# RWKV-6 attention and a maxout layer on one core: one step loop with helpers, against a tabled order of single operations

## The chip, the cores and the metric

One core of one Trainium2 chip runs the kernel. The time is that of the device in microseconds; 199.82 is the median of three runs of the kernel before. The engines are TensorE (PE; its weight loads are PEld), VectorE (DVE), ScalarE (ACT), GpSimd (POOL) and SyncE (SP), which here issues transfers. Each engine works its own queue in order.

## The reference

```python
for t in range(S):                       # attention: B=4, H=8, S=768, D=48
    cur = np.einsum('bhd,bhe->bhde', u[None] * kt, vt)
    y[:, :, t] = np.einsum('bhd,bhde->bhe', rt, state + cur)
    state = wt[:, :, :, None] * state + np.einsum('bhd,bhe->bhde', kt, vt)
...
h1 = x @ w1                              # maxout: x is [3072, 384], w1 and w2 [384, 1024]
h2 = x @ w2
g = np.maximum(h1, h2)
return (g @ w_out).astype(np.float32)
```

Here x is the attention's y with the heads of a token side by side.

## The kernel before

The sequence is cut into chunks of 256 positions. A unit n is one chunk of one batch: chunk n // 4 of batch n % 4, so there are 12 units, and unit n needs the state that unit n-4 left. Partition p of a unit's tiles holds positions 2p and 2p+1 of the chunk.

What a unit goes through, by the names in the code:
- `load` (L80): w, k, r and v, 384 KB each, on SP's queue; 4 buffers each.
- `logw`: lw = ln w (ACT), lp = sum of the two positions (POOL). `cumsum`: one matmul with a triangle (PE, PSUM `ex`), the exponential A (ACT), mz (DVE). `exps`: A and iA (ACT). `scale_rk`: rkn, r and k times the decays (DVE).
- `bonus_mul` and `bonus_sum`: vb, rku = r k u (POOL), its row sums dg (DVE), vd (POOL).
- `transp`: 8 transposes of rkn for r and 8 for k through one PSUM buffer `tr`, and the copies rT and kT (DVE). `kv`: 32 small matmuls to PSUM `y`, then S and Tf (DVE).
- `scores`, twice: 16 matmuls to one PSUM buffer `sc` and the masked copy M (DVE). `y_inter`, `y_intra`: the output in PSUM `y`, copied to x (ACT). `xt`: transposes and the copy xT (ACT).
- `gate` j = 0 to 3: 6 matmuls of xT with wd = w1 - w2 to `go` (two PSUM buffers), a Relu to gT (ACT). With max(h1, h2) = relu(h1 - h2) + h2 the second term goes through wc = w2 w_out.
- `outp` b = 0, 1: 3 matmuls with wc and 8 with w_out, the copy osb (ACT, 4 buffers) and the store of 192 KB (SP, L368), whose target is written as two interleaved sets of 64 rows.
- `decay_row`, `decay_load`: one row of mz goes to DRAM (row, L212) and comes back spread over partitions (WL, L219); `decay_exp`, `decay`: the state S_f and S_0 of the batch (ACT, POOL).

The weights: w1 on SP (L90), w2 and w_out on POOL's queue (L137), w2 turned by three DMA transposes on SP (L145, `weights_turn`), wd by three subtractions (DVE, L141), wc by 24 matmuls (L151, `weights_out`).

The schedule is manual: an engine gets its instructions in the order in which the Python code calls the helpers. `step` lays attention of unit a (first half), unit t (second half), the gates of g and the outputs of o past one another, helper by helper; the calls at the end start the first units and then run `step(n, n-1, n-2, n-2)`. A helper holds the work of several engines, so their orders are bound to one another.

Of the kernel before, what the change touches and what calls it, by code (L numbers as in the profile page):

```python
# [12 lines left out]
AX = mybir.AxisListType  # L13

# [20 lines left out]
def _body(tc, r, k, v, w, u, moe_w1, moe_w2, moe_w_out, out):  # L35
    nc = tc.nc
    B, H, S, D = r.shape
    P = 128
# [9 lines left out]
    NU = NC * B  # L48

# [3 lines left out]
    ldp = tc.alloc_tile_pool(name="ld", bufs=4)  # L53
# [18 lines left out]

    L = {}

    def load(n):
        c, b = unit(n)
        d = {}
        for name, src in (("w", w), ("k", k), ("r", r), ("v", v)):
            t = ldp.tile([P, H, 2, D], F32, tag="l" + name, name="l" + name)
            nc.sync.dma_start(  # L80
                out=t.rearrange("p h i d -> p h (i d)"),
                in_=src[b, :, c * C:(c + 1) * C, :].rearrange("h (p i) d -> p h (i d)", i=2))
            d[name] = t
        L[n] = d

    load(0)
    u_b = const.tile([P, HD], F32)
    nc.sync.dma_start(out=u_b, in_=u.rearrange("h d -> (h d)").partition_broadcast(P))
    w1f = const.tile([P, KO, d_ff], F32)
    nc.sync.dma_start(out=w1f, in_=moe_w1.rearrange("(o p) n -> p o n", p=P))  # L90


# [4 lines left out]
    triI = const.tile([P, P], F32)  # L97
    mask = const.tile([P, 2, 2, Q], F32)
    sel = const.tile([P, 2, 2, Q], BF16)

    def constants():
        make_upper_triangular(nc, triI, val=1.0, diag=True)
        nc.gpsimd.memset(sel, 0.0)
        for b in range(2):
            q = slice(b * Q, (b + 1) * Q)
            for i in range(2):
                nc.gpsimd.tensor_copy(sel[q, i, i, :], ident[q, q])
                for i2 in range(2):
                    nc.gpsimd.tensor_copy(mask[q, i, i2, :],
                                          (triI if (i, i2) == (0, 1) else triS)[q, q])  # L110

    NRK = 2
    MZ = [const.tile([P, 2, H, DP], F32, name=f"mz{i}") for i in range(2)]
    rkn_b = [const.tile([P, 2, 2, H, DP], BF16, name=f"rkn{i}") for i in range(NRK)]
# [9 lines left out]
    for b in range(B):  # L124
        nc.vector.memset(S_f[b], 0.0)
    for t in S_0 + S_1:
        nc.gpsimd.memset(t, 0.0)


    wd_sb = const.tile([P, KO, d_ff], BF16)  # L130
# [5 lines left out]
    def weights_load(src, dst):  # L136
        nc.gpsimd.dma_start(out=dst, in_=src.rearrange("(o p) n -> p o n", p=P))  # L137

    def weights_gate():
        for ko in range(KO):  # L140
            nc.vector.tensor_sub(wd_sb[:, ko, :], w1f[:, ko, :], w2_sb[:, ko, :])  # L141

    def weights_turn():
        for ko in range(KO):
            nc.sync.dma_start_transpose(out=w2T_sb[:, ko], in_=w2_sb[:, ko, :])  # L145

    def weights_out():
        for ko in range(KO):
            wc_p = pt_([P, HD], F32, "go", 2)
            for fo in range(FO):  # L150
                nc.tensor.matmul(wc_p, w2T_sb[:, ko, fo, :],  # L151
                                 wo_sb[:, fo, :], start=(fo == 0), stop=(fo == FO - 1))
            nc.vector.tensor_copy(wc_sb[:, ko, :], wc_p)


    U = {}
# [4 lines left out]
    def logw(n):  # L161
        s = U[n] = {}
        s["lw"] = lw = wt_([P, H, 2, D], F32, "lw")
        nc.scalar.activation(lw, L[n]["w"], AF.Ln)  # L164
        s["lp"] = lp = wt_([P, H, D], F32, "lp")
        nc.gpsimd.tensor_add(lp, lw[:, :, 0, :], lw[:, :, 1, :])  # L166

    def bonus_mul(n):
        s = U[n]
        s["vb"] = vb = wt_([P, H, 2, D], BF16, "vb", 3)  # L170
        nc.gpsimd.tensor_copy(vb, L[n]["v"])
        s["rku"] = rku = wt_([P, H, 2, D], F32, "rku", 1)
        nc.gpsimd.tensor_mul(rku, L[n]["r"], L[n]["k"])  # L173
        nc.gpsimd.tensor_mul(  # L174
            byi(rku), byi(rku),
            u_b.rearrange("p (h d) -> p h d", h=H).unsqueeze(1).to_broadcast([P, 2, H, D]))

    def bonus_sum(n):
        s = U[n]
        dg = wt_([P, H, 2, 1], F32, "dg")  # L180
        nc.vector.reduce_sum(dg, s["rku"], axis=AX.X)  # L181
        s["vd"] = vd = wt_([P, 2, H, D], BF16, "vd", 3)
        nc.gpsimd.tensor_mul(byi_inv(vd), L[n]["v"], dg.to_broadcast([P, H, 2, D]))  # L183

    def byi_inv(t):
        return t.rearrange("p i h d -> p h i d")

    def cumsum(n):
        s = U[n]
        lw, lp = s["lw"], s["lp"]  # L190
# [9 lines left out]
    def exps(n):  # L200
        s = U[n]
        mz = s["mz"]
        nc.scalar.activation(s["A"][:, 1], mz[:, 0, :, 0:D], AF.Exp)
        s["iA"] = iA = wt_([P, 2, H, D], F32, "iA", 1)
        nc.scalar.activation(iA, mz[:, :, :, 0:D], AF.Exp, scale=-1.0)

    def decay_row(n):
        if last(n):
            return
        s = U[n]  # L210
        s["row"] = row = drp.tile([1, H * DP], F32, tag="row", name="row")
        nc.sync.dma_start(out=row, in_=s["mz"][P - 1:P, 1].rearrange("b h d -> b (h d)"))  # L212

    def decay_load(n):
        if last(n):
            return
        s = U[n]
        s["WL"] = wl = wt_([P, NP], F32, "WL")
        nc.sync.dma_start(out=wl, in_=s["row"].rearrange("b (p x) -> x (b p)", x=P))  # L219

    def scale_rk(n):
        s = U[n]
        s["rkn"] = rkn = rkn_b[n % NRK]
        nc.vector.tensor_mul(rkn[:, 0, :, :, 0:D], byi(L[n]["r"]), s["A"])
        nc.vector.tensor_mul(rkn[:, 1, :, :, 0:D], byi(L[n]["k"]), s["iA"])  # L225
# [12 lines left out]

    def decay_exp(n):
        if last(n):  # L240
            return
        s = U[n]
        s["Wt"] = wt = wt_([P, NP, 1], F32, "Wt")
        nc.scalar.activation(wt.rearrange("p q o -> p (q o)"), s["WL"], AF.Exp)

    def kv(n):

        s = U[n]
        b = unit(n)[1]
# [12 lines left out]
        for e in range(2):
            q = slice(e * DP, (e + 1) * DP)
            nc.vector.tensor_add(S_1[n % 2][q, :, e * D:(e + 1) * D],  # L264
                                 kp[q, 0, 0:NP * D].rearrange("p (q d) -> p q d", d=D), S_f[b][q])
        if not last(n):
            nc.vector.tensor_add(T_f[b].rearrange("p q d -> p (q d)"), kp[:, 1, 0:NP * D],
                                 S_f[b].rearrange("p q d -> p (q d)"))

    def decay(n):  # L270
        if last(n):
            return
        b = unit(n)[1]
# [192 lines left out]
```

## Time and profile before

| | us |
|---|---|
| median of 3 runs (199.71 to 200.17) | 199.82 |
| the profiled execution | 199.22 |
| its span, first to last instruction | 197.5 |
| PE busy / POOL / DVE / ACT | 146.2 / 101.9 / 108.3 / 88.1 |
| transfers of 8 KB and less on SP's queue: share of the 16 DMA engines' span | 49.6% |

In the profile SP's issuing of transfers is not busy time, so SP has to be read from the timeline and its waits. A DMA share is the mean over sixteen DMA engines, so two busy ones show as about 0.13. Matmul ends are modelled: a group of matmuls shows some 0.15 us longer than the distance to the next group's start.

### The profile page before, as it was taken

Reading aid. Unit: us, or ns where it says so; the run is one execution under the profiler, and the core shown is the slowest. Engines: PE = TensorE matmul, PEld = TensorE weight load, DVE = VectorE, ACT = ScalarE, POOL = GpSimd, SP = SyncE. Lnnn points to the kernel's source line nnn. Section 1 sums busy time; section 2 is a strip of 40 time slices with the busy share of each in tenths; the row PEclk is TensorE's granted clock in tenths of the full one; section 3 lists DMA queues with packets and bytes.
Section 4 is the critical chain, followed back from the end, with each engine's and each line's share of the span. In section 5 each row is a group of like instructions: output and inputs, shape, how many; then the busy total and the mean of one; then the engine's idle time right before and its main releaser. Section 6 shows DMA issues by size and latency. Waiting matters only on the chain.

```text
span 197.5 us, 4973 instructions
## 1 busy us (share of the span) xinstructions
PE 146.2 (74%) x2080; PEld 100.3 (51%) x2080; DVE 108.3 (55%) x154; ACT 88.1 (45%) x153; POOL 101.9 (52%) x115
## 2 busy tenths in 40 slices
PE   0325543674998998989989899898998989997900
PEld 0114321443566665666757667566675666755500
DVE  3245840777827758477583774847748477540000
ACT  4300122705058364583645826558365572535400
POOL 6996002996196294782946929469295642000000
PEclk9999999999699999999999999999999999999965
DMA  6995999979414826646549366473571110101110
GB/s 172 325 297 95 140 174 325 269 199 319 124 26 125 229 75 184 185 124 168 135 130 240 79 168 179 120 208 95 162 209 53 42 53 14 46 35 36 49 42 35
DMA packets 62454, 28.07 MB, mean 142 GB/s; under 512 B 57432, under 2 KB 61656, under 8 KB 62432
## 3 DMA queue, kind: packets, MB, share of 16 engines
q1 hardware_dynamic: 60992, 26.19, 49.6%
q0 software_dynamic: 1440, 1.57, 5.1%
q8 instruction: 16, 0.26, 0.5%
q14 instruction: 6, 0.05, 0.1%
HBM read 23.81 MB, written 4.73 MB: 145 GB/s over the span
## 4 chain that ended last, share of the span: by engine, by line
PE 40%; DVE 19%; POOL 9%; ACT 9%; DMA 8%; issue 6%; SPq 3%; DVEq 0%; POOLq 0%; ACTq 0%
PE go L362 13%; DVE M L291 7%; PE go L359 6%; PE go L347 5%; DMA w_sb<-in_moe_w_dram 4%; DVE S L264 4%; SPq L145 3%; DMA lw<-in_w_dram 3%; PE ex L192 3%; ACT xT L337 3%; PE sc L288 2%; ACT osb L365 2%; PE y L323 2%; DVE rkn L225 2%; PE y L302 2%
## 5 line engine op out<-in xcount | busy, mean ns | idle before, releaser
L347 PE MATMUL go<-xT,wd_sb 128*128 128x256 bf16 x288 | 38.5, 279 | 6.8 <-ACT xT L337 6.7
L183 POOL TENSOR_TENSOR vd<-lv,dg 128x768 bf16<-128x768 f32 x12 | 17.7, 1477 | 41.7 <-DVE dg L181 41.7
L347 PEld LDWEIGHTS <-wd_sb 128*128 128x128 bf16 x288 | 27.9, 100 | 16.7 <-issue 10.2
L362 PE MATMUL go<-wo_sb,gT 128*128 128x384 bf16 x192 | 35.4, 328 | 0.0
L351 ACT ACTIVATE gT<-go 128x512 bf16<-128x512 f32 x48 | 27.4, 591 | 14.4 <-PE go L347 14.2
L291 DVE TENSOR_TENSOR M<-sc,mask 128x1024 bf16<-128x1024 f32 x24 | 29.3, 1222 | 6.8 <-PE sc L288 6.7
L365 ACT COPY osb<-go 128x384 f32<-128x384 f32 x24 | 11.5, 479 | 44.7 <-PE go L362 44.7
L362 PEld LDWEIGHTS <-gT 128*128 128x128 bf16 x192 | 18.9, 99 | 12.8 <-issue 0.5
L174 POOL TENSOR_TENSOR rku<-rku,u_b 128x768 f32<-128x768 f32 x12 | 22.4, 1870 | 0.9
L166 POOL TENSOR_TENSOR lp<-lw 128x384 f32<-128x384 f32 x12 | 12.7, 1056 | 19.6 <-ACT lw L164 19.6
L173 POOL TENSOR_TENSOR rku<-lr,lk 128x768 f32<-128x768 f32 x12 | 22.4, 1866 | 0.0
L232 PE MATMUL tr<-ident,rkn 128*128 128x128 bf16 x192 | 15.5, 226 | 9.1 <-DVE rT L237 6.4
L192 PE MATMUL ex<-lp,triS 128*128 128x384 f32 x24 | 11.9, 583 | 10.7 <-POOL lp L166 10.7
L237 DVE COPY rT<-tr 128x1024 bf16<-128x1024 bf16 x12 | 8.3, 690 | 20.9 <-PE tr L232 20.9
L288 PE MATMUL sc<-rT,kT 48*64 48x128 bf16 x384 | 10.9, 231 | 11.6 <-DVE M L291 11.6
L232 PEld LDWEIGHTS <-rkn 128*128 128x128 bf16 x192 | 12.8, 101 | 10.9 <-issue 5.9
L197 DVE TENSOR_TENSOR mz<-ex,lw 128x384 f32<-128x384 f32 x12 | 6.7, 558 | 19.2 <-ACT A L196 19.2
L359 PE MATMUL go<-wc_sb,xT 128*128 128x384 bf16 x72 | 16.2, 336 | 0.0
L328 ACT CAST x<-y 128x768 bf16<-128x768 f32 x12 | 9.6, 799 | 14.3 <-PE y L323 13.9
L237 DVE COPY kT<-tr 128x1024 bf16<-128x1024 bf16 x12 | 8.3, 692 | 12.4 <-PE tr L232 12.4
L288 PEld LDWEIGHTS <-kT 48*64 48x64 bf16 x384 | 7.9, 112 | 13.9 <-issue 13.6
L225 DVE TENSOR_TENSOR rkn<-lk,iA 128x768 bf16<-128x768 f32 x12 | 13.7, 1138 | 0.0
(51 smaller groups left out, 194.9 us busy)
## 6 DMA issues: line engine op xcount, KB each, us to landing
lw<-in_w_dram SPq DMA_DIRECT2D x12, 384.0 KB
lk<-in_k_dram SPq DMA_DIRECT2D x12, 384.0 KB
lr<-in_r_dram SPq DMA_DIRECT2D x12, 384.0 KB
lv<-in_v_dram SPq DMA_DIRECT2D x12, 384.0 KB
out_dram<-osb SPq DMA_DIRECT2D x24, 192.0 KB
w1f<-in_moe_w_dram SPq DMA_DIRECT2D x1, 1536.0 KB
w_sb<-in_moe_w_dram POOLq DMA_DIRECT2D x1, 768.0 KB, 8.0
wo_sb<-in_moe_w_out_dram POOLq DMA_DIRECT2D x1, 768.0 KB, 10.7
```

The costliest lines, as they stand in the source:

```text
L173: nc.gpsimd.tensor_mul(rku, L[n]["r"], L[n]["k"])
L174: nc.gpsimd.tensor_mul(byi(rku), byi(rku), u_b.rearrange("p (h d) -> p h d", h=H).unsqueeze(1).to_broadcast([P, 2, H, D]))
L183: nc.gpsimd.tensor_mul(byi_inv(vd), L[n]["v"], dg.to_broadcast([P, H, 2, D]))
L192: nc.tensor.matmul(ex, triS, lp.rearrange("p h d -> p (h d)"))
L225: nc.vector.tensor_mul(rkn[:, 1, :, :, 0:D], byi(L[n]["k"]), s["iA"])
L232: nc.tensor.transpose(tp[:, p, :, i, :], s["rkn"][:, x, i, 2 * p:2 * p + 2, :].rearrange("s r d -> s (r d)"), ident)
L288: nc.tensor.matmul(sc[q, e, p, :], kT[d, p, b, i, :], rT[d, p, b])
L291: nc.vector.tensor_mul(M.rearrange("s e p t -> s (e p) t"), sc.rearrange("s e p t -> s (e p) t"), mask[:, i].rearrange("s i q -> s (i q)") ...
L347: nc.tensor.matmul(g[:, f, :], wd_sb[:, ko, fo * P:(fo + 1) * P], s["xT"][:, ko].rearrange("p j t -> p (j t)"), start=(f == 0 and ko == 0) ...
L351: nc.scalar.activation(s["gT"][:, 2 * j:2 * j + 2].rearrange("p f j t -> p f (j t)"), g, AF.Relu)
L359: nc.tensor.matmul(o, s["xT"][:, ko, b, :], wc_sb[:, ko, :], start=(ko == 0), stop=False)
L362: nc.tensor.matmul(o, s["gT"][:, fo, b, :], wo_sb[:, fo, :], start=False, stop=(fo == FO - 1))
```

## The change

The helpers are split so that each operation issues work on one engine, under a short name, and a table `ORDER` gives all of them with their unit, one after another. `step`, and the calls that started the first units, are gone. A loop reads the table:

```diff
+ORDER = """
+w.0 k.0 lw.0 lp.0 cs.0 r.0 u v.0 w2 rk.0 rku.0 vb.0 AE.0 z.0 m.0 AO.0 rp.0 tr.0 iA.0 kp.0 evr.0
...
+xT.6 kv.7 Tf.7 S1.7 ob0.5 oc1.5 os0.5 out0.5 oa1.5 ob1.5 g0.6 rk.8 rku.8 k.11 r.11 tr.8 evr.8
...
-    ldp = tc.alloc_tile_pool(name="ld", bufs=4)
+    LB = 3
+    ldp = tc.alloc_tile_pool(name="ld", bufs=LB)
...
-                nc.gpsimd.tensor_copy(sel[q, i, i, :], ident[q, q])
-                for i2 in range(2):
-                    nc.gpsimd.tensor_copy(mask[q, i, i2, :],
+                nc.vector.tensor_copy(sel[q, i, i, :], ident[q, q])
+                for i2 in range(2):
+                    nc.vector.tensor_copy(mask[q, i, i2, :],
...
-    for t in S_0 + S_1:
-        nc.gpsimd.memset(t, 0.0)
+    for t in S_f + S_1 + S_0:
+        nc.vector.memset(t, 0.0)
...
+    def wcm(ko):
+        WC[ko] = t = pt_([P, HD], F32, "go", 2)
+        for fo in range(FO):
+            nc.tensor.matmul(t, w2T_sb[:, ko, fo, :], wo_sb[:, fo, :],
+                             start=(fo == 0), stop=(fo == FO - 1))
+
+    @op
+    def wce(ko):
+        nc.vector.tensor_copy(wc_sb[:, ko, :], WC[ko])
...
-        s["xT"] = xT = wt_([P, KO, 2, P], BF16, "xT")
-        nc.scalar.copy(xT, tp)
+        U[n]["xT"] = t = wt_([P, KO, 2, P], BF16, "xT", 3)
+        nc.scalar.copy(t, U[n]["xt"])
...
-        osb = wt_([P, HD], F32, "osb", 4)
-        nc.scalar.copy(osb, o)
+        U[n]["s", b] = t = wt_([P, HD], F32, "osb", 5)
+        nc.scalar.copy(t, U[n]["o", b])
...
+    for name in ORDER.split():
+        name, _, n = name.partition(".")
+        OP[name](int(n or 0))
```

The short names: cs is the cumsum's matmul, AE and AO the two halves of A, m and z the two of mz, rp and kp rkn for r and k, tr/evr and tk/evk the transposes and their copies, sc/M the scores, yb, yi and ya the three parts of y, wcm/wce the matmuls and the copy of wc, wt a DMA transpose, g/r a gate and its Relu, oc, oa and ob the parts of an output with wc and the two halves of gT, os and out its copy and its store, dec and S0 the state. The vd tile has 2 buffers where it had 3. No matmul, transfer, activation or POOL operation of a unit is added or taken out.

The first place is the start of SP's queue, behind the loads of unit 0 (lw, lk, lr, lv are the loaded w, k, r, v; a number is a tile of its own). Before:

```order
L90 DMA w1f_82<-in_moe_w1_dram 128x3x1024
L145 DMA_TRANSPOSE w2T_sb_132<-w2_sb_130 128x8x128 x3
L80 DMA lw_168<-in_w_dram 128x8x96
L80 DMA lk_170<-in_k_dram 128x8x96
L80 DMA lr_172<-in_r_dram 128x8x96
L80 DMA lv_174<-in_v_dram 128x8x96
L80 DMA lw_176<-in_w_dram 128x8x96
```

Now:

```order
L272 DMA row_250<-mz0_90 1x512
L190 DMA w1f_135<-in_moe_w1_dram 128x3x1024
L176 DMA lw_283<-in_w_dram 128x8x96
L176 DMA lk_287<-in_k_dram 128x8x96
L176 DMA lr_289<-in_r_dram 128x8x96
L176 DMA lv_291<-in_v_dram 128x8x96
L176 DMA lw_298<-in_w_dram 128x8x96
L272 DMA row_308<-mz1_91 1x512
L206 DMA_TRANSPOSE w2T_sb_139<-w2_sb_137 128x8x128
L176 DMA lk_362<-in_k_dram 128x8x96
```

The transposes, which need the loaded w2, stood ahead of every load of unit 1; now unit 1's loads and w of unit 2 are ahead of the first of them, and ahead of it stands the row of unit 1.

The second place is SP's queue in the middle, one unit. Before, the two outputs stand together, then WL and row:

```order
L368 DMA out_0_dram<-osb_601 2x64x384
L368 DMA out_0_dram<-osb_655 2x64x384
```

Now (an output's number rises with the time):

```order
L272 DMA row_913<-mz0_90 1x512
L500 DMA out_0_dram<-osb_1008 2x64x384
L176 DMA lk_1032<-in_k_dram 128x8x96
L176 DMA lr_1034<-in_r_dram 128x8x96
L277 DMA WL_1047<-row_913 128x4x1
L500 DMA out_0_dram<-osb_1072 2x64x384
L176 DMA lv_1110<-in_v_dram 128x8x96
```

Of one unit's two outputs the second now stands behind k, r and WL, and v, w and row follow before the next unit's first.

The third place is ScalarE's queue, one unit in the middle. Before (x is the attention's output, xT its transpose, gT a Relu):

```order
L365 COPY osb_1361<-go_1349 128x384
L328 CAST x_1396<-y_1330 128x768
L244 ACTIVATE Wt_1398<-WL_1162 128x4
L365 COPY osb_1415<-go_1403 128x384
L337 COPY xT_1429<-ex_1422 128x768
L351 ACTIVATE gT_1450<-go_1451 128x512
L196 ACTIVATE A_1472<-ex_1470 128x384
```

Now:

```order
L446 CAST x_1411<-y_1366 128x768
L241 ACTIVATE A_1416<-ex_1413 128x384
L253 ACTIVATE A_1416<-mz0_90 128x384
L474 ACTIVATE gT_1334<-go_1442 128x512
L258 ACTIVATE iA_1458<-mz0_90 128x768
L458 COPY xT_1468<-ex_1461 128x768
L495 COPY osb_1514<-go_1450 128x384
```

The copy xT, which the next gate needs, stood behind the copies of both outputs of the unit before; now it stands ahead of both, and between x and xT there are the exponentials of the next unit and a Relu.

## Rows read from the trace of the kernel before

**Rows 1.** The page's busy time by engine: us, share of the span, instructions.

```profile
PE 146.2 (74%) x2080; PEld 100.3 (51%) x2080; DVE 108.3 (55%) x154; ACT 88.1 (45%) x153; POOL 101.9 (52%) x115
```

**Rows 2.** Chain: start, us, what. Window: PE, PEld, DVE, ACT, POOL, clock, DMA share, GB/s.

```profile
56.38 0.48 ACT osb L365
...
57.61 0.81 PE go L347 x6
...
70.01 0.81 PE go L347 x6
...
187.25 0.48 ACT osb L365
...
57.61:187.25 129.64, 117.02 (x1744) 82.17 (x1743) 78.36 (x111) 71.66 (x127) 68.46 (x65) 1.00 0.44 120
```

**Rows 3.** The timeline of SP's issues in one round: start, us, line, target and source.

```profile
118.41 2.46 SPq L368 DMA_DIRECT2D out_dram<-osb  x2
...
125.00 0.38 SPq L80 DMA_DIRECT2D lw<-in_w_dram  x1
...
131.35 1.13 SPq L368 DMA_DIRECT2D out_dram<-osb  x1
```

**Rows 4.** Windows: loads alone, one round, outputs alone; columns as in rows 2.

```profile
30.54:35.50 4.96, 2.74 (x9) 1.58 (x10) 0.53 (x2) 1.82 (x3) 1.97 (x3) 1.00 1.17 325
118.41:131.35 12.94, 11.79 (x187) 8.41 (x186) 8.34 (x12) 7.43 (x14) 8.47 (x9) 1.00 0.58 157
190.00:196.00 6.00, 0.00 (x0) 0.00 (x0) 0.00 (x0) 0.00 (x0) 0.00 (x0) 0.50 0.13 50
```

**Rows 5.** What SP's queue waited for: us in all, times, longest.

```profile
SPq L368 <- ACT osb L365: 49.0, 14, 9.3
SPq L145 <- DMA w_sb<-in_moe_w_dram: 11.3, 1, 11.3
SPq L461 <- DMA out_dram<-osb: 8.0, 2, 4.1
```

**Rows 6.** Windows in which the DMA engines stood still or had only outputs.

```profile
16.10:18.40 2.30, 1.33 (x22) 1.13 (x23) 1.20 (x3) 0.00 (x0) 1.90 (x2) 1.00 0.06 10
18.40:30.00 11.60, 6.20 (x110) 3.97 (x106) 7.24 (x9) 1.60 (x2) 0.46 (x1) 1.00 1.18 166
38.70:41.00 2.30, 2.26 (x14) 1.36 (x14) 2.30 (x2) 0.47 (x1) 2.30 (x2) 1.00 0.07 1
51.40:56.00 4.60, 4.60 (x54) 2.54 (x52) 2.72 (x4) 1.38 (x3) 1.80 (x2) 0.85 0.03 8
156.00:196.00 40.00, 27.79 (x369) 19.23 (x366) 12.62 (x17) 15.44 (x27) 5.86 (x5) 0.92 0.12 40
```

**Rows 7.** The timeline of the first w, its use on ScalarE, and unit 1's row.

```profile
0.74 0.45 SPq L80 DMA_DIRECT2D lw<-in_w_dram  x1
4.11 0.84 ACT L164 ACTIVATE lw<-lw 128x768 f32<-128x768 f32 x1 [2.09 <-DMA lw<-in_w_dram]
...
30.79 0.84 ACT L164 ACTIVATE lw<-lw 128x768 f32<-128x768 f32 x1 [4.14 <-DMA lw<-in_w_dram]
...
35.50 1.11 SPq L212 DMA_DIRECT2D row<-mz  x1
```

**Rows 8.** The timeline of TensorE behind one gate; in brackets the idle time before.

```profile
119.92 0.82 PE L347 MATMUL go<-xT,wd_sb 128*128 128x256 bf16 x6 [0.49 <-ACT xT L337]
120.57 0.61 PE L232 MATMUL tr<-ident,rkn 128*128 128x128 bf16 x8
121.02 0.86 PE L192 MATMUL ex<-lp,triS 128*128 128x384 f32 x2
...
122.47 0.80 PE L257 MATMUL y<-vb,rkn 64*64 64x48 bf16 x32
...
125.69 0.42 PE L288 MATMUL sc<-rT,kT 48*64 48x128 bf16 x16 [0.66 <-DVE M L291]
```

**Rows 9.** The groups by line on POOL: the mask copies.

```profile
L109 POOL COPY mask<-triS 64x64 f32<-64x64 f32 x6 | 1.3, 239 | 0.0
```

More of the change, by code (lines that the diff above doesn't have):

```diff
@@ L69, in last @@
         return unit(n)[0] == NC - 1
[L73 to L90, printed above, removed]
     triS = const.tile([P, P], F32)
@@ L134, in _body @@
     wc_sb = const.tile([P, KO, HD], BF16)
[L136 to L153, printed above, removed]
@@ L156, in _body, with op, rows @@
-    U = {}
+    U = [{} for _ in range(NU)]
+    OP = {}
+    def op(f):
+        OP[f.__name__] = f
+        return f
+    def rows(t):
+        return t.rearrange("(o p) n -> p o n", p=P)
     def byi(t):
         return t.rearrange("p h i d -> p i h d")
[L161 to L166, printed above, removed]
@@ L200, in exps @@
[L200 to L212, printed above, removed]
@@ L214, in decay_load, with load @@
[L214 to L225, printed above, removed]
+    def load(n, name, src):
+        c, b = unit(n)
+        U[n][name] = t = ldp.tile([P, H, 2, D], F32, tag="l" + name, name="l" + name)
+        nc.sync.dma_start(
+            out=t.rearrange("p h i d -> p h (i d)"),
+            in_=src[b, :, c * C:(c + 1) * C, :].rearrange("h (p i) d -> p h (i d)", i=2))
@@ new lines, in _body, with u, w1, w2 @@
+    for name, src in (("w", w), ("k", k), ("r", r), ("v", v)):
+        OP[name] = lambda n, name=name, src=src: load(n, name, src)
+    @op
+    def u(n):
+        nc.sync.dma_start(out=u_b, in_=u_in.rearrange("h d -> (h d)").partition_broadcast(P))
+    @op
+    def w1(n):
+        nc.sync.dma_start(out=w1f, in_=rows(moe_w1))
+    @op
+    def w2(n):
+        nc.gpsimd.dma_start(out=w2_sb, in_=rows(moe_w2))
+    @op
+    def wo(n):
+        nc.gpsimd.dma_start(out=wo_sb, in_=rows(moe_w_out))
@@ L354, in outp, with relu, out_c @@
-    def outp(n, b):
-        c, b0 = unit(n)
-        s = U[n]
-        o = pt_([P, HD], F32, "go", 2)
+    def relu(n, j):
+        if j == 0:
+            U[n]["gT"] = wt_([P, FO, 2, P], BF16, "gT")
+        nc.scalar.activation(
+            U[n]["gT"][:, 2 * j:2 * j + 2].rearrange("p f j t -> p f (j t)"), U[n]["g", j],
+            AF.Relu)
+    for j in range(4):
+        OP[f"g{j}"] = lambda n, j=j: gate(n, j)
+        OP[f"r{j}"] = lambda n, j=j: relu(n, j)
+    def out_c(n, b):
+        U[n]["o", b] = t = pt_([P, HD], F32, "go", 2)
@@ L428, in _body, with out_s, out_d @@
-    for n in range(3, NU + 2):
-        if n + 2 < NU:
-            load(n + 2)
-        step(n if n < NU else None, n - 1 if n - 1 < NU else None, n - 2, n - 2)
+    def out_s(n, b):
+        U[n]["s", b] = t = wt_([P, HD], F32, "osb", 5)
+        nc.scalar.copy(t, U[n]["o", b])
+    def out_d(n, b):
+        c, bb = unit(n)
+        tok = bb * S + c * C + b * P
+        nc.sync.dma_start(out=out[tok:tok + P, :].rearrange("(q i) n -> i q n", i=2),
+                          in_=U[n]["s", b])
+    for b in range(2):
+        OP[f"oc{b}"] = lambda n, b=b: out_c(n, b)
+        OP[f"oa{b}"] = lambda n, b=b: out_g(n, b, 0)
+        OP[f"ob{b}"] = lambda n, b=b: out_g(n, b, 1)
+        OP[f"os{b}"] = lambda n, b=b: out_s(n, b)
+        OP[f"out{b}"] = lambda n, b=b: out_d(n, b)
```

353 lines of the change are left out of this document (200 added, 153 removed).

## Prediction

> **What bounds the kernel now.** I read the page's shares by engine first [rows 1]: TensorE is busy for 146.2 of 197.5 us (74%) and no other engine for more than 55%. Taken alone that says "TensorE, with gaps". The windows put a size on it [rows 2]: between the first gate matmul of unit 1 at 57.61 and the last output copy at 187.25 TensorE is busy for 117.02 of 129.64 us. So 12.6 us of gaps lie in the steady part, and the other loss is the start: 57.6 us before the steps run one after another.
>
> The third view is SP's queue [rows 3], and it says something else. From 118.41 to 131.35 eight transfers, two outputs, WL, row and four loads, are issued one behind the other with no gap of over 0.15 us, then come the outputs of the next unit: 12.94 us for the round. TensorE's own steps are shorter: 12.4 us from the gate at 57.61 to the next unit's at 70.01 [rows 2]. So SP does not wait for the engines here; it is held by the transfers. Why, the windows tell [rows 4]. Where only outputs are under way (190 to 196) the share is 0.13, two of sixteen DMA engines, at 50 GB/s: 128 x 384 x 4 B = 196.6 KB take 196.6 / 50 = 3.93 us. Where only loads are (30.54 to 35.50), all sixteen run at 325 GB/s: 393.2 KB take 1.21 us. The waits of SP agree: of the last two outputs it waits 8.0 us in two waits, the longer 4.1 [rows 5]. Now 2 x 3.93 + 4 x 1.21 = 12.70, and the round takes 12.94; 0.24 is left for row and WL. The times add up as if in one line, and on the two engines that carry outputs they are: each load also has a sixteenth of its bytes there. These two engines are full in that stretch, and all 48 loads, 24 outputs and the weights must pass through them. They are the second bound, one that no share on the page shows.
>
> So the question for this change is where those two engines stand idle [rows 6]: 16.1 to 18.4 us (SP stands at the transposes until the gate weights have landed, 11.3 us [rows 5]), 38.7 to 41.0 (SP waits for the landing of row), 51.4 to 56.0 (the loads have run out of buffers and no output is ready), and in 156 to 196 only outputs are left and they wait for TensorE: 40 GB/s instead of 50.
>
> **The change part by part.**
> *Transfers.* Their number, shapes and engines stay as they were; their order and their waits change. Idle that can go: 2.3 us at share 0.06 of 1.17 is 2.2; 2.3 at 0.07 is 2.2; 4.6 at 0.03 is 4.5; 40 x (1 - 40/50) is 8.0. Together 16.9. If all of it goes, the span is 197.5 - 16.9 = 180.6. Taking each in turn:
> - 16.1 to 18.4 goes: behind unit 0's loads SP now has w1, the four loads of unit 1 and w of unit 2, which need no engine. The next wait is row of unit 1, ahead of the first transpose. It needs w of unit 1 landed (at about 19, below), then lw, lp, cs, m, AO, rp, z. Before, that row was issued 4.7 us after lw began, at 30.79 and 35.50 [rows 7], and rp now stands ahead of z, 1.0 us: 24.7. The loads ahead last until about 22.5 and POOL's load of w_out fills what follows. Idle there between 0 and 3; I take 0.5.
> - 38.7 to 41.0 goes: WL of units 1 and 0 come after three loads and three transposes, so their rows have landed. WL of unit 2 follows row by two loads, 2.4 us of transfers in the queue while SP waits. Idle between 0 and 2; I take 0.2.
> - 51.4 to 56.0 goes if the first outputs are ready when the queue reaches them. Ahead of them are 25 loads (30.3 us), u, w1 and w2 (3.34 MB at 325 GB/s, 10.3), and w_out with the transposes, which filled 18.4 to 30 but for one load (10.4) [rows 6]: from 2.7 the line reaches them at about 54. The outputs are ready at about 48 (below).
> - 156 to 196 goes if TensorE is ahead by then (below).
> - Against these, the transposes and w_out ran at 18.4 to 30 partly alone; with loads queued between them about 1 us may come back (between 0 and 2). I take 1.0.
> Sum: 180.6 + 0.5 + 0.2 - 1.0 = 180.3 us of span. The profiled execution took 199.22 for 197.5, so 1.7 lie around it: **182.0**. That execution is 0.6 below the median of the runs; I leave this out, since it is a third of a per cent.
>
> *TensorE's line.* It decides only where it is later than the transfers. Its start: w of unit 1 lands at 30.79 before [rows 7]. In the new queue only 4 x 393 + 197 + 2 x 1573 KB stand ahead of it, 15.1 us at 325 GB/s from about 2.7, so it lands at about 19, some 12 us earlier; the empty queue's own delay is seen in the first load, issued at 0.74 and used at 4.11. VectorE gives some back: three wd subtractions and the masks of unit 0 now stand ahead of unit 1's m. I take 9 of 12 (bounds 0 and 12): gate 0 of unit 1 at 57.6 - 9 = 48.6, and the first output copied just ahead of it, as it was at 56.38 before [rows 2]. By then it has also done some work that stood behind that gate: transposes, cumsum, kv and half of the scores of the next units, 0.61 + 0.86 + 0.80 + 0.42 = 2.7 us by rows of their kind [rows 8]. Then 117.0 - 2.7 = 114.3 us of work without gaps ends at 162.9, with all of the old gaps at 175.5. The gaps were waits for ScalarE's xT behind osb (0.49) and VectorE's mask M (0.66) [rows 8]. In the new order six groups of matmuls lie between x and xT's use and four between the two score halves, against copies of 0.5 to 1.2 us, so I expect most to go: 165. From the last matmul group's copy at 187.25 to the end of the transfers took 8.8 us; 165 + 8.8 = 173.8, under the 178.8 at which the two engines are through. TensorE's gain is therefore mostly not seen: it would wait at the end as a line of outputs behind it.
>
> *Fewer load buffers (4 to 3), more osb (4 to 5).* A round of transfers is 12.9, a round of TensorE perhaps 11.2, for six rounds in which both loads and outputs run; the transfers fall behind by up to 10 us. The loads are issued three units ahead (33 us), osb holds two and a half units, so nobody waits; only w of unit 11 comes close, 1 to 2 us which the end hides. Were that cover gone, ScalarE stands at lw and all behind it.
>
> *Constants.* The selector and mask copies and the zeroing of the states move from POOL to VectorE: 12 copies of 0.24 [rows 9] and some memsets, done at about 6, ahead of the first z at 8.3, so nothing; uncovered, 3 us.
>
> *A figure that speaks otherwise.* The outputs' rate is measured here at 50 GB/s on two engines [rows 4]. The Trainium skill (DMA: Bandwidth & Descriptors, Specifications) gives about 27 GiB/s for an engine, 58 GB/s for two. By that an output would take 3.4 us and the estimate would fall by 24 x 0.5, to 169; the row decides, and it shows less.
>
> **The rivals.**
> 1. *TensorE's line stays the later one.* The start is won but the gaps are not, since waits move to new places: 175.5 + 8.8 + 1.5 + 1.7 = 187.5. For it: VectorE and POOL are each busy for 8.4 of 12.9 us in a unit [rows 4], and in a fixed order one late step stalls all behind it on its engine. Against it: 170.0 + 8.8 is the transfers' end, so TensorE would have to end after 170.0, with over half of the old gaps left.
> 2. *The two engines do not bind.* SP's unbroken issue would then be a habit of its queue and the outputs faster when asked: 165 + 8.8 + 1.5 + 1.7 = 177. Against it: the tail at 50 GB/s and the sum of 12.7.
> 3. *Slower.* The place is SP's queue at k of unit n+3, which may only go out once POOL's rku of unit n has read the old k, now with one buffer fewer, and which stands ahead of an output. If the engines lose their lead of some 7 us over SP there, SP stands in each of six units while the two engines run empty, and each restart costs an empty queue's delay of 3.4 us (0.74 to 4.11): 6 x 3.4 = 20.4, so 180.3 + 20.4 + 1.7 = 202.4. It needs more than 2.9 us per unit to come out slower than before. For it: k, r and WL now stand between a unit's two outputs. Against it: the start gives the lead first.
>
> **How the numbers follow.** The forecast 0.75, rival 1 0.14, rival 2 0.06, rival 3 0.05. The time is that of the forecast, 182.0. Its own bounds are the idle that I could not see: from 179 (nothing new, 2 us back) to 185.5. The range for 8 in 10 goes from 178.5 to 187.0 and takes in most of rival 1. About 0.2% is what a measurement here tells from no change. All cases but rival 3 are faster, and of its 0.05 a fifth, where the stops are near 2.9 us each, lies at the old time: faster 0.95, within 0.2% 0.01, slower 0.04.
>
> **What would show it.** Right: after about 56 us the windows show a DMA share that never falls under 0.13 and 50 GB/s to the end; outputs are copied (osb) well ahead of their issue, with SP's waits for osb (49.0 us before [rows 5]) nearly gone from the last 40 us; TensorE ends 10 us or more before the end of the transfers; w of unit 1 is used at about 19. Wrong: holes of over 1 us in the DMA row between 56 us and the end, SP waiting for POOL or ScalarE in mid-kernel, or a last osb within 9 us of the end, which is rival 1.

## The result, and the profile after

| | before | changed |
|---|---|---|
| median of the runs | 199.76 us (199.57 to 200.17, 4 runs) | 190.57 us (189.69 to 190.74, 4 runs) |
| ratio, 95% interval | | 0.9528 (0.9496 to 0.9561) |
| span of the profiled execution | 197.5 us | 188.8 us |
| first and last osb (copy of an output) begin at | 56.38, 187.25 us | 54.76, 177.04 us |

The change is 9.2 us faster. The prediction had 17.8 (182.0, range 178.5 to 187.0): direction right, size about twice what came. A median takes in all executions of a run and a ratio leaves out the slowed ones: by those alone the runs given below at 187.35, 196.36, 197.19 and 175.95 us have 187.33, 196.16, 196.40 and 175.49.

The page's line that answers to [rows 1]: TensorE's work is nearly the same (148.2 for 146.2 us), on a shorter span. VectorE is busy for 124.8 us where it was 108.3. Little of that is work taken over: its two products rkn take 20.0 and 19.3 us in all where they took 11.6 and 13.7, which is 14.0 of the 16.5 us (the last section shows one of them).

```profile
PE 148.2 (78%) x2080; PEld 102.7 (54%) x2080; DVE 124.8 (66%) x173; ACT 88.3 (47%) x153; POOL 106.4 (56%) x96
```

The windows of the changed kernel answer to [rows 2, 4]. Columns: stretch, us, busy time of PE, PEld, DVE, ACT, POOL, granted clock, DMA share, GB/s.

```profile
57.30:177.04 119.74, 114.40 (x1663) 80.74 (x1662) 85.03 (x101) 69.60 (x124) 74.55 (x64) 1.00 0.42 116
76.00:81.00 5.00, 5.00 (x73) 3.67 (x68) 4.94 (x7) 3.01 (x6) 4.92 (x4) 1.00 0.20 39
78.00:79.00 1.00, 1.00 (x9) 0.66 (x7) 1.00 (x1) 0.54 (x2) 1.00 (x2) 1.00 0.08 23
79.00:80.00 1.00, 1.00 (x14) 0.85 (x12) 1.00 (x2) 0.81 (x2) 1.00 (x2) 1.00 0.16 1
137.00:187.00 50.00, 34.92 (x454) 24.22 (x450) 16.01 (x19) 18.99 (x32) 15.61 (x12) 0.92 0.14 51
```

From gate 0 of unit 1 to the last osb TensorE now works 114.40 of 119.74 us, where it was 117.02 of 129.64. In the last 50 us the DMA share is 0.14 at 51 GB/s to the end: only outputs, two engines, always busy, as forecast. The three rows between are the surprise: after 76 us the transfers run dry, and from 79 to 80 they move 1 GB/s. SP's waits say why (these answer to [rows 5]; columns: who waits for whom, us, times, longest):

```profile
SPq L500 <- ACT osb L495: 29.1, 9, 7.4
SPq L272 <- DVE mz L249: 11.8, 2, 7.5
SPq L542 <- DMA out_dram<-osb: 9.6, 3, 4.3
...
SPq L277 <- ACT Wt L282: 5.6, 1, 5.6
```

And SP's own issues, where these waits lie (start us, us, line; they answer to [rows 3]):

```profile
20.21 1.15 SPq L176 DMA_DIRECT2D lw<-in_w_dram  x1
28.97 0.25 SPq L272 DMA_DIRECT2D row<-mz  x1
...
69.68 0.53 SPq L500 DMA_DIRECT2D out_dram<-osb  x1
70.32 0.47 SPq L176 DMA_DIRECT2D lk<-in_k_dram  x1
70.84 2.08 SPq L176 DMA_DIRECT2D lr<-in_r_dram  x1
78.57 0.37 SPq L277 DMA_DIRECT2D WL<-row  x1
78.99 0.52 SPq L500 DMA_DIRECT2D out_dram<-osb  x1
```

SP stands twice: at row of unit 1 (L272) until 28.97, and at WL of unit 4 (L277) until 78.57. The second is a buffer: WL has two, so unit 4's may be written only once Wt of unit 2 has read its own. ScalarE's timeline has that Wt just ahead of it:

```profile
78.35 0.19 ACT L282 ACTIVATE Wt<-WL 128x4 f32<-128x4 f32 x1
```

The order gives out Wt.2 only between the WLs of units 5 and 6. With all loads, outputs and rows behind one another in SP's queue, everything stands with it.

TensorE's line has a stall of its own. POOL stands 9.5 us at vb of unit 11, which the order gives out one round early, beside vb of unit 9; its v was issued at 132.55. vd of unit 9 stands behind it, and TensorE waits for that. POOL's and TensorE's rows (start us, us, ..., in brackets the idle time before and its releaser):

```profile
140.02 0.82 POOL L288 CAST vb<-lv 128x768 bf16<-128x768 f32 x1 [9.49 <-DMA lv<-in_v_dram]
140.80 1.47 POOL L309 TENSOR_TENSOR vd<-lv,dg 128x768 bf16<-128x768 f32 x1
```

```profile
142.32 0.51 PE L413 MATMUL y<-vd,sel 64*128 64x384 bf16 x4 [2.71 <-POOL vd L309]
...
148.84 0.43 PE L352 MATMUL y<-vb,rkn 64*64 64x48 bf16 x16 [2.02 <-POOL vb L288]
```

So both lines have lost time: TensorE's, whose last osb is at 177.04, and that of the transfers, with which the span ends at 188.8. Which of the two sets the time can't be read from that; the experiments decide.

### The profile page after: what moved, and what is told of

The parts are those of the page before. It is cut to its first block, busy times and chain, and to the rows that moved or that the text cites. A ratio compares the mean times of both kernels' runs of the same rounds, so it can differ in the third digit from the quotient of the medians.

```text
span 188.8 us, 4945 instructions
## 1 busy us (share of the span) xinstructions
PE 148.2 (78%) x2080; PEld 102.7 (54%) x2080; DVE 124.8 (66%) x173; ACT 88.3 (47%) x153; POOL 106.4 (56%) x96
## 4 chain that ended last, share of the span: by engine, by line
PE 54%; issue 6%; POOL 5%; DMA 4%; DVE 2%; ACT 2%; SPq 1%; DVEq 0%; POOLq 0%; ACTq 0%
PE go L466 14%; PE go L490 14%; PE go L485 5%; PE tr L317 4%; DMA lw<-in_w_dram 4%; PE y L352 3%; PE ex L235 3%; PE sc L393 3%; PE y L437 2%; PE y L413 2%; PE go L214 2%; PE y L425 2%; PE ex L453 2%; POOL rku L293 1%; POOL rku L298 1%
## 5 line engine op out<-in xcount | busy, mean ns | idle before, releaser
L466 PE MATMUL go<-xT,wd_sb 128*128 128x256 bf16 x288 | 40.1, 285 | 0.9 <-ACT xT L458 0.9
L490 PE MATMUL go<-wo_sb,gT 128*128 128x384 bf16 x192 | 36.8, 326 | 0.0
L230 POOL TENSOR_TENSOR lp<-lw 128x384 f32<-128x384 f32 x12 | 16.9, 1411 | 17.9 <-ACT lw L225 17.9
L298 POOL TENSOR_TENSOR rku<-rku,u_b 128x768 f32<-128x768 f32 x12 | 24.1, 2010 | 0.9
L262 DVE TENSOR_TENSOR rkn<-lr,A 128x768 bf16<-128x768 f32 x12 | 20.0, 1664 | 2.1 <-ACT A L253 2.1
L266 DVE TENSOR_TENSOR rkn<-lk,iA 128x768 bf16<-128x768 f32 x12 | 19.3, 1604 | 1.3 <-ACT iA L258 1.3
L288 POOL CAST vb<-lv 128x768 bf16<-128x768 f32 x12 | 11.3, 943 | 9.9 <-DMA lv<-in_v_dram 9.5
L225 ACT ACTIVATE lw<-lw 128x768 f32<-128x768 f32 x12 | 10.1, 844 | 13.2 <-DMA lw<-in_w_dram 13.2
L446 ACT CAST x<-y 128x768 bf16<-128x768 f32 x12 | 9.6, 796 | 11.6 <-PE y L437 11.4
L241 ACT ACTIVATE A<-ex 128x384 f32<-128x384 f32 x12 | 5.9, 490 | 18.1 <-DVE mz L245 11.6
L304 DVE TENSOR_REDUCE dg<-rku 128x16 f32<-128x768 f32 x12 | 11.3, 944 | 3.1 <-POOL rku L298 3.1
```

The lines of the kernel that those rows point to most:

```text
L262: nc.vector.tensor_mul(rkn_b[n % 2][:, 0, :, :, 0:D], byi(U[n]["r"]), U[n]["A"])
L266: nc.vector.tensor_mul(rkn_b[n % 2][:, 1, :, :, 0:D], byi(U[n]["k"]), U[n]["iA"])
L298: nc.gpsimd.tensor_mul(t, t, u_b.rearrange("p (h d) -> p h d", h=H).unsqueeze(1).to_broadcast([P, 2, H, D]))
L466: nc.tensor.matmul(g[:, f, :], wd_sb[:, ko, fo * P:(fo + 1) * P], U[n]["xT"][:, ko].rearrange("p j t -> p (j t)"), start=(f == 0 and ko == ...
L490: nc.tensor.matmul(U[n]["o", b], U[n]["gT"][:, fo, b, :], wo_sb[:, fo, :], start=False, stop=(fo == FO - 1))
```

## The experiments

Two theories at the start. Theory 1, the prediction's: the two DMA engines that carry the outputs set the time, and the missing 8.6 us are idle time or transfers on their line. Theory 2: TensorE's line sets it, and the outputs are only its tail. Each run is compared with runs of the kernel before on the same chip (its medians were 199.36 to 199.47 us); the changed kernel's own time is 190.57, and a difference between two runs is good to 1 to 1.5 us.

**Take TensorE's stall away, leave the transfers.** In the order, `lw.11 lp.11` and `vb.11` move to their usual places:

```diff
-... tk.9 evk.9 vb.9 lw.11 lp.11
-r2.7 vb.11 dg.9 vd.9 ...
+... tk.9 evk.9 vb.9
+r2.7 dg.9 vd.9 ...
-... sc1.9 M1.9 Wt.7 ...
+... sc1.9 M1.9 lw.11 lp.11 Wt.7 ...
-... tk.11 evk.11 r0.9 ...
+... tk.11 evk.11 vb.11 r0.9 ...
```

> The changed kernel with lw, lp and vb of unit 11 given out at the same place in the round as those of the other units, so that POOL no longer stands 9.5 us for v of unit 11 ahead of vd of unit 9. Theory 1: TensorE's gaps from 136 to 150 us (about 5 us) go, but the outputs still leave at the two engines' pace, so the time falls by 0 to 1, to 189.5 to 190.6. Theory 2: the last output is copied about 5 us earlier and the time falls by 4 to 5, to about 186.

189.91 us, ratio 0.9499 (0.9449 to 0.9548). The last osb of this run, on ScalarE's timeline:

```profile
171.76 0.48 ACT L495 COPY osb<-go 128x384 f32<-128x384 f32 x1 [1.63 <-PE go L490]
```

TensorE is 5.3 us earlier (171.76 for 177.04), the time 0.7, which is inside the interval of some 1 us. Theory 2 falls for the changed kernel: five microseconds of TensorE's time were hidden behind the outputs.

**Free the two engines.** Each output goes out as two transfers of 64 rows:

```diff
-        nc.sync.dma_start(out=out[tok:tok + P, :].rearrange("(q i) n -> i q n", i=2),
-                          in_=U[n]["s", b])
+        dst = out[tok:tok + P, :].rearrange("(q i) n -> i q n", i=2)
+        for i in range(2):
+            nc.sync.dma_start(out=dst[i], in_=U[n]["s", b][i * Q:(i + 1) * Q, :])
```

> The changed kernel with each output stored by two DMAs of 64 rows instead of one whose outermost dimension is 2. Theory 1: such a store is shared by all sixteen DMA engines, moves at about 300 GB/s, and the DMA line stops to bind; TensorE's line is left, its stalls for late loads gone too, last copy at about 171 and the end at 174 to 178. Theory 2: the middle stays as it is (last copy at about 177) and only the tail behind it is shorter, 8 to 9 us less: 180 to 183. If the stores stay on two engines, the time stays at 190 or grows by the 24 added issues.

177.72 us, ratio 0.8877 (0.8820 to 0.8935): 12.9 us less than the changed kernel. The first row is that of all its stores, the second ScalarE's last osb, the third a window from 57.30 on:

```profile
DMA to landing us min/median/max: 2.1/2.2/4.2
```

```profile
171.78 0.48 ACT L495 COPY osb<-go 128x384 f32<-128x384 f32 x1 [1.35 <-PE go L490]
```

```profile
57.30:171.00 113.70, 113.48 (x1659) 80.29 (x1658) 85.19 (x101) 69.43 (x123) 75.09 (x64) 1.00 0.48 124
```

A store of half an output lands 2.2 us after its issue, the tail behind the last osb is 4.3 us (176.1 - 171.8), and TensorE works 113.48 of 113.70 us. In this kernel TensorE is the bound, and its stall for v of unit 11 is gone too, since v comes in time.

**The same edit on the kernel before.**

> The kernel before with the same stores in two halves. Theory 1, by which before was still held in mid-kernel by the transfers (12.94 us a round against 12.4 of TensorE's): the round falls little, since TensorE's own gaps remain, and the tail of 8.8 us behind the last copy falls to about 2.5: 191 to 194. If the old round was held by the transfers alone: also 0.5 us in each of 10 rounds, 187 to 189. If the stores stay on two engines: 199.5 to 201.

193.63 us, ratio 0.9693 (0.9634 to 0.9752). SP's outputs of two units, and the last osb on ScalarE's timeline:

```profile
91.52 3.70 SPq L369 DMA_DIRECT2D out_dram<-osb  x4
...
104.05 3.50 SPq L369 DMA_DIRECT2D out_dram<-osb  x4
```

```profile
187.03 0.48 ACT L365 COPY osb<-go 128x384 f32<-128x384 f32 x1 [1.31 <-PE go L362]
```

SP's round is now 12.53 us, near the 12.4 of the engines' steps [rows 2], where it was 12.94 [rows 3]. The last osb stays where it was (187.25); only the tail shrinks. So in the kernel before the transfers did not hold the rounds, the engines' 12.4 did, and the two merely ran level. With the stores out of the way the new order is worth 193.63 - 177.72 = 15.9 us; with them on two engines it shows 9.2.

**Is it the shape or the number of transfers?** Two transfers again, but cut by columns, so that the outermost dimension stays 2:

```diff
+        for n0 in range(0, HD, HD // 2):
+            nc.sync.dma_start(out=dst[:, :, n0:n0 + HD // 2], in_=U[n]["s", b][:, n0:n0 + HD // 2])
```

> The changed kernel with each output stored by two DMAs too, but cut by columns (2 x 64 x 192 each), so that the outermost dimension stays 2. Theory 1 in the form that the outermost dimension decides how many engines carry a store: still two engines at 50 GB/s or less, 190 to 194 (below 50 GB/s if rows of 768 bytes are carried less well). The rival, that two transfers in flight are what helped the stores by halves of rows: about 178.

196.36 us, ratio 0.9838 (0.9769 to 0.9907), above the 194 that theory 1 allowed. A window of outputs alone:

```profile
150.00:180.00 30.00, 29.52 (x361) 20.16 (x359) 10.22 (x13) 15.64 (x27) 8.58 (x7) 1.00 0.14 48
```

Two engines still, at 48 GB/s in place of 51. At these rates an output takes 4.10 us for 3.85, and 24 of them 5.8 more, which is what the time rose by (196.36 - 190.57). Two transfers alone don't help: it is the shape. The Trainium skill (DMA: Bandwidth & Descriptors, Rules for kernel authors) says that the slowest dimension sets how many engines carry a transfer, and an outermost dimension of 2 confines it to two; both stores agree (share 0.14 of sixteen with 2 x 64 x 384, 2.2 us to land with 64 x 384). The same list advises against cutting a transfer into halves of the partitions, since both use the same sixteen engines; here the halves won 12.9 us, because the whole did not use sixteen.

**Is it SP's queue?** Outputs issued from ScalarE, with four WL buffers:

```diff
-        nc.sync.dma_start(out=out[tok:tok + P, :]...
+        nc.scalar.dma_start(out=out[tok:tok + P, :]...
```

> The changed kernel with four WL buffers and its outputs issued from ScalarE's queue in place of SP's. Theory 1 (the engines, not the queue, hold the outputs): 186.5 to 189.5, no faster than the 187.35 of the same kernel with outputs on SP, the two-engine share of 0.13 unbroken at the end; ScalarE may lose time where its issues stand behind a full queue. The rival (SP's one queue holds loads and outputs behind one another): loads and outputs pass each other and the time falls below 183.

197.19 us, ratio 0.9882 (0.9807 to 0.9958), slower than either theory had it. SP's waits hold something new:

```profile
SPq L176 <- DMA out_dram<-osb: 13.2, 2, 10.5
```

By the profile SP's loads now wait for landings of outputs (13.2 us), a wait that isn't among SP's in the changed kernel. It gives no gain to the rival, but the new wait keeps it from being a clean test.

**The stand at WL.** One word:

```diff
-        U[n]["WL"] = t = wt_([P, NP], F32, "WL")
+        U[n]["WL"] = t = wt_([P, NP], F32, "WL", 4)
```

> The changed kernel with four WL buffers in place of two, so that the issue of unit 4's WL no longer waits for Wt of unit 2. Theory 1 (the two DMA engines that carry the outputs set the time): the 5.6 us stand of SP at WL goes, the DMA line starts again some 5 to 6 us earlier, and the time falls by 4.5 to 6, to 184.5 to 186. Theory 2 (TensorE's late line sets it, the outputs' tail hangs behind it): only what an earlier v of unit 11 gives TensorE's gaps shows, 1 to 3 us, 187.5 to 189.5. If SP then just stands at the next thing that isn't ready: no change.

187.35 us, ratio 0.9355 (0.9297 to 0.9413): 3.2 less, not the 4.5 to 6 of theory 1. SP's rows:

```profile
70.24 2.15 SPq L176 DMA_DIRECT2D lr<-in_r_dram  x1
72.48 3.18 SPq L277 DMA_DIRECT2D WL<-row  x1
75.79 0.58 SPq L500 DMA_DIRECT2D out_dram<-osb  x1
```

The output behind WL is issued at 75.79 for 78.99: 3.2 us earlier, which is what the time fell by. The rest of the 5.6 us was no loss, since the engines were still working off what SP had issued ahead: here too the issue of WL takes 3.18 us, until there is room.

**The stand at row of unit 1**, moved behind the first transpose and the loads of unit 2:

```diff
-... v.1 lp.1 wd.1 wd.0 wo w.2 cs.1 AE.1 m.1 AO.1 rp.1 z.1 row.1 wd.2 rk.1 ...
+... v.1 lp.1 wd.1 wd.0 wo w.2 cs.1 AE.1 m.1 AO.1 rp.1 z.1 wd.2 rk.1 ...
-... v.2 w.3 wt.0 wt.2 ...
+... v.2 w.3 row.1 wt.0 wt.2 ...
```

> The changed kernel with SP's row of unit 1 moved behind the first transpose and the loads of unit 2, so that SP doesn't stand from 21.4 to 29.0 us for z of unit 1. Theory 1 (the line of the two engines stood partly idle there): the loads of unit 2 land some 5 us earlier beside the load of w_out, the outputs' line starts 2.5 to 5 us earlier and the time falls by as much, to 185.5 to 188. Theory 3 (w_out's load fills all engines until 29.6 whatever else is queued; the shares of 0.9 to 1.26 in the windows there say so): 0 to 1.5, 189 to 190.6.

189.72 us, ratio 0.9516 (0.9444 to 0.9587): 0.9 us less, inside the interval, and theory 3's number. SP now issues the transpose at 22.63 for 29.31, but the first output at 57.28 for 56.07. SP's stand of 7.5 us cost little, since w_out kept the engines busy: the share was 1.01 from 18.4 to 30 in the changed kernel, where [rows 6] had 1.18:

```profile
18.40:30.00 11.60, 5.38 (x67) 3.10 (x60) 7.79 (x8) 3.39 (x5) 7.95 (x5) 1.00 1.01 201
```

**What do row and WL take on the line?** Their transfers left out, with a constant in WL's place:

```diff
-        nc.sync.dma_start(out=t, in_=MZ[n % 2][P - 1:P, 1].rearrange("b h d -> b (h d)"))
...
-        U[n]["WL"] = t = wt_([P, NP], F32, "WL")
-        nc.sync.dma_start(out=t, in_=U[n]["row"].rearrange("b (p x) -> x (b p)", x=P))
+        U[n]["WL"] = wl0
```

> The changed kernel without the eight row and eight WL transfers; Wt is computed from a constant instead, so the decay of the state is not the reference's. Theory 1: the 3.2 us that the stand at unit 4's WL cost go, and the line is shorter by what the pairs take on it. At 0.24 us a pair, as the prediction had it: 190.6 - 3.2 - 1.9 = 185.5. At 0.7 a pair, the 13.4 us rounds of the changed kernel less 12.70 for outputs and loads: 190.6 - 3.2 - 5.6 = 181.8. The rival, that the rounds are longer because loads and outputs slow each other: 186 to 187.4.

185.67 us, ratio 0.9335 (0.9284 to 0.9387), just what 0.24 us a pair gives. With WL alone left out:

> As the run without row and WL, but row is still written and only WL is left out. If WL, 512 elements of 4 bytes, is what a pair costs: within 1 us of the run without both. If row, one write of 2 KB, is: 2.5 to 4.5 us above it, near 186 to 187.

186.27 us, ratio 0.9364 (0.9306 to 0.9422), 0.6 above. But both runs carry a disturbance. In 44 to 50 us, where loads are under way and no output yet, the window of the run without both is the first row, that of the changed kernel the second:

```profile
44.00:50.00 6.00, 5.67 (x95) 3.56 (x95) 4.44 (x8) 2.55 (x6) 3.25 (x3) 1.00 1.28 261
```

```profile
44.00:50.00 6.00, 6.00 (x66) 3.65 (x65) 3.90 (x7) 2.23 (x4) 2.41 (x3) 0.85 1.16 321
```

The loads are a fifth slower. What is new ahead of them is the constant of 16 bytes per partition, which shifts the tiles allocated behind it. Once the outputs run the slow loads hardly show: SP's outputs end 12.8 us a round apart without both (102.99 and 115.77) and 13.0 to 13.2 with row alone (90.34, 103.29, 116.46). To rule the shift out the constant was made 256 bytes:

```diff
-    wl0 = const.tile([P, NP], F32)
+    wl1 = const.tile([P, 16 * NP], F32)
+    wl0 = wl1[:, 0:NP]
```

> As the run without row and WL, but the constant that takes WL's place fills 256 bytes of a partition instead of 16, so that all tiles behind it stand at their old alignment. In the run with 16 bytes the loads of the stretch 44 to 50 us moved at 261 GB/s, in the changed kernel at 321. Theory A (the shift of 16 bytes slowed the loads and hid what row and WL cost): 320 GB/s again, rounds of 12.0 to 12.7 us, and a time of 180 to 183. Theory B (row and WL cost 0.24 us a pair, loads were slower for another reason): 185 to 186, 261 GB/s again.

183.41 us, ratio 0.9198 (0.9158 to 0.9238): theory A, 0.4 above its bound. The same window, then SP's first outputs and three of them one round apart:

```profile
44.00:50.00 6.00, 5.67 (x85) 3.54 (x82) 4.12 (x8) 2.65 (x6) 3.24 (x3) 1.00 1.17 325
```

```profile
53.35 2.30 SPq L501 DMA_DIRECT2D out_dram<-osb  x2
...
95.85 2.65 SPq L501 DMA_DIRECT2D out_dram<-osb  x1
...
108.22 3.00 SPq L501 DMA_DIRECT2D out_dram<-osb  x1
...
121.02 2.91 SPq L501 DMA_DIRECT2D out_dram<-osb  x1
```

Against the changed kernel's:

```profile
92.40 0.59 SPq L500 DMA_DIRECT2D out_dram<-osb  x1
...
105.92 0.59 SPq L500 DMA_DIRECT2D out_dram<-osb  x1
...
119.32 0.61 SPq L500 DMA_DIRECT2D out_dram<-osb  x1
...
129.54 2.91 SPq L500 DMA_DIRECT2D out_dram<-osb  x1
```

An issue ends when the queue has room, so I compare the ends: 98.50, 111.22, 123.93 without the pair, rounds of 12.72 and 12.71; 92.99, 106.51, 119.93 with it, 13.52 and 13.42. Two outputs and four loads are 12.70. A pair of row and WL, 4 KB in all, takes 0.7 to 0.8 us. The changed kernel's own trace agrees: its next round holds no pair, and its end, 132.45, comes 12.52 behind 119.93.

The changed kernel with four WL buffers takes 187.35 us, this one 3.9 less. That is not the pairs' transfers alone, for SP's waits at row and WL went with them: this run's first two outputs are issued by 55.65, the other's by 57.84, so 2.2 us are won before any of these rounds. With the constant of 16 bytes it is 58.53, which is where the slow loads cost.

And the shift alone, an unused tile of 16 bytes:

> The changed kernel with nothing but an unused tile of 16 bytes per partition ahead of the states' tiles, written once by VectorE. Theory A: the loads of 44 to 50 us move at 260 GB/s instead of 321, 48 loads take some 0.3 us more each on the two output engines where these are full: 4 to 12 us longer, 195 to 202. Theory B: no change, 189.5 to 191.

190.82 us, ratio 0.9554 (0.9505 to 0.9602): no change in time, theory B's number, but theory A's rate in the window. Its window, and SP's rows:

```profile
44.00:50.00 6.00, 5.68 (x95) 3.57 (x95) 4.89 (x9) 3.01 (x6) 3.24 (x3) 1.00 1.27 263
```

```profile
58.71 1.24 SPq L502 DMA_DIRECT2D out_dram<-osb  x2
...
76.36 3.46 SPq L279 DMA_DIRECT2D WL<-row  x1
79.86 0.57 SPq L502 DMA_DIRECT2D out_dram<-osb  x1
```

The first outputs go out 2.6 us later (58.71 for 56.07), the output behind WL of unit 4 only 0.9 later (79.86 for 78.99): the slower loads eat the hole that the stand at WL left. So a loss ahead of an idle stretch need not show in the time. Its later rounds, 13.49 to 13.54, are like the changed kernel's: where outputs run too the slower loads cost nothing, which theory A had wrong.

**Does an earlier start help?** w of unit 1 ahead of w1 (`yi.0 w.1 w1 lw.1`), with four WL buffers and row of unit 1 moved:

> The changed kernel with four WL buffers, row of unit 1 moved and w of unit 1 loaded ahead of w1, so that unit 1's first step on ScalarE can begin some 3 us earlier. Theory 1 in the form that the two engines have been carrying transfers since 2.7 us without a pause: an earlier start of the engines changes nothing, 186 to 187.5 as with WL alone. If the first outputs' copy (54.8 us) is what starts the line of outputs: 2 to 3 us less, 184 to 185.5.

187.79 us, ratio 0.9409 (0.9360 to 0.9457), as with the WL buffers alone. ScalarE's lw of unit 1 begins at 16.50 for 20.19, yet the first osb comes at 55.46 for 54.76. All edits with the stores spread, without and with that one:

> All four edits together on the changed kernel: stores in two halves of 64 rows, four WL buffers, lw, lp and vb of unit 11 in their usual place, row of unit 1 moved. Theory 1: with the stores spread the DMA line no longer binds, TensorE's line does (177.7 for the stores alone), and the other edits give only what TensorE's start gains from loads that land earlier: 0 to 3, 174.5 to 177.7. If the DMA line bound still, WL and row would add their 3 and 2.5 to 5: 170 to 172.

> All four edits and w of unit 1 loaded ahead of w1, with the stores spread. TensorE's line binds there, so an earlier start of unit 1 shows whole: 2 to 3 us under 176.3, 173 to 174.5. If something else than w of unit 1 holds TensorE's start (the masked scores, the gate weights' differences that wait for w1): 176 to 177.

176.26 us, ratio 0.8884 (0.8810 to 0.8958), and 175.95 us, ratio 0.8807 (0.8768 to 0.8846). Both within the interval of the spread stores alone or just beside it: once TensorE is the bound, the edits on SP's queue buy 0 to 2 us. These, and the one edit on the stores at 177.72, are the fastest of all.

## Why the prediction was wrong, and where it was right

The missing 8.6 us (190.57 - 182.0), by runs: 3.2 from the wait for a WL buffer (190.57 to 187.35). Another 3.9 go when row and WL are left out (187.35 to 183.41), but the forecast held eight pairs too, at its own 0.24 each 1.9 us; so only about 2.0 of these belong to the miss. Some 3.4 stay open.

- *The two DMA engines set the time.* Right. The store's shape moves the time by 12.9 us, TensorE's 5.3 us by 0.7. The share of 0.14 at 51 GB/s holds to the end, and the last osb stands 11.8 us ahead of the span's end (188.8 - 177.04, "10 us or more"). One sign was badly chosen: SP still waits 29.1 us for osb, since it issues an output as soon as it is copied, and the transfers queue behind the issue. The price of an output and of a load was right to 0.02 us a round (12.72 for 12.70).
- *The step that failed is the term for the stands of SP* ("idle between 0 and 2; I take 0.2" for the WLs). It looked at row and WL as a wait for data and never asked how many buffers WL has and when the order gives out its reader. Named as a sign of being wrong (holes of over 1 us, SP waiting for ScalarE in mid-kernel), it came: 5.6 us of stand, 3.2 of loss where 0.2 had been taken.
- *The 0.24 us "left for row and WL"* did not hold in the new order: there a pair takes 0.7 to 0.8. In the old order it can hardly have been more, since a round of 12.94 held a pair beside the same outputs and loads, which take 12.72 without one; a round that the engines paced as well can only have been longer than the transfers needed. So a second step failed with the first: the forecast says of the transfers that "their order and their waits change" and gives the new order the old price. Row and WL stood next to each other and now stand apart, between outputs and loads; why that costs more was not tried.
- *"So SP does not wait for the engines here; it is held by the transfers."* Half wrong: with the stores spread the old round only falls to 12.5, and the last osb doesn't move. Two bounds stood level.
- *16.1 to 18.4, 0.5 for row of unit 1.* The row was issued at 28.97, not at 24.7: lw of unit 1 began 1.2 us later than taken, and on the way to z POOL's lp took 1.93 us and VectorE's rp 2.02, each about twice its short form. So SP's stand was sized far too small; but the cost, 0.9 us by the run and within its noise, was about right, and for a reason that was given: w_out filled the engines.
- *TensorE's lead of 9 of 12 us.* Wrong: gate 0 of unit 1 came at 57.30, not at 48.6; only the lower bound, 0, held. w of unit 1 was there on time (lw at 20.19 for "about 19"). An earlier one, at 16.50, brought no earlier osb, so something behind it holds the start; what, no run tells. The work of 114.3 us was right (114.40), and so was that most gaps go: without the stall 57.30 + 114.40 = 171.7 is where the last osb comes (171.76). The stall itself was not foreseen: the text had 1 to 2 us at w of unit 11, and it was v, for an operation that the order gives out a round early. That "the end hides" it was right, 5.3 us of it.
- *The rivals.* Rival 1 at 187.5 lay nearest, by chance: its mechanism, TensorE's line, was not the cause. Rival 3, SP standing in mid-kernel, was the right kind of mishap at the wrong place, WL and not k, once and not in each unit.

## What to carry to other kernels

Before an order is trusted, go along each in-order queue and ask of every instruction with few buffers where the reader of its old buffer stands; one such wait in a queue that all loads share stops everything behind it. What a stand costs is read from the next output's issue, not from the wait's length: engines that still have work behind it hide part of it. And look at how many DMA engines a transfer uses before its bandwidth is taken as given; a store whose outermost dimension is 2 cost this kernel 12.9 us, more than any one place of the order that was tried here.

## What the runs showed that was not expected

- Moving the tiles behind a constant by 16 bytes per partition slowed loads that run without outputs from 321 GB/s to between 261 and 263, in three runs; a shift of 256 bytes left them at 325. No other shift was tried.
- Two transfers of 2 KB, one of them in elements of 4 bytes, hold up a full line for 0.7 to 0.8 us in the new order, more than half of a load of 393 KB (1.21); in the old order, next to each other, they left a round of 12.94 room for some 0.2.
- VectorE's product rkn of r and A, one form, takes 0.95 us or up to 2.60 in the same execution; before, it took 0.95 or 0.96 in eleven of twelve units. The groups before and now (us in all, then mean ns), two of VectorE's rows of the changed kernel, and POOL's beside the second:

```profile
L224 DVE TENSOR_TENSOR rkn<-lr,A 128x768 bf16<-128x768 f32 x12 | 11.6, 968 | 0.9 <-ACT A L203 0.8
```

```profile
L262 DVE TENSOR_TENSOR rkn<-lr,A 128x768 bf16<-128x768 f32 x12 | 20.0, 1664 | 2.1 <-ACT A L253 2.1
```

```profile
41.39 0.95 DVE L262 TENSOR_TENSOR rkn<-lr,A 128x768 bf16<-128x768 f32 x1
...
98.79 2.59 DVE L262 TENSOR_TENSOR rkn<-lr,A 128x768 bf16<-128x768 f32 x1
```

```profile
96.86 1.81 POOL L293 TENSOR_TENSOR rku<-lr,lk 128x768 f32<-128x768 f32 x1
98.75 1.81 POOL L298 TENSOR_TENSOR rku<-rku,u_b 128x768 f32<-128x768 f32 x1
```

The short one began when POOL's rku had just ended (39.38 + 1.80 = 41.18); the long one began 0.04 us after a POOL product of 1.81 us, and 1.81 + 0.95 is 2.76. The Trainium skill (SBUF — State Buffer, SBUF: two separate sides) says that the two engines share a pair of ports, which the first takes for the whole instruction; the rows agree. No run here tried it by itself. It is one candidate for why the start did not come earlier: rkn of unit 1 took 2.02 us, and nothing was moved to test that.
